# One-hot blocks of a token list: 24 packed blocks, one instruction each, in place of four instructions over a strided table

## The chip, the core and the metric

The kernel runs on one NeuronCore of a Trainium2 chip. TensorE (PE) multiplies matrices, VectorE (DVE) and ScalarE (ACT) work on elements, GpSimd (POOL) does elementwise work and issues the indirect DMAs, SyncE (SP) issues the other DMAs. The metric is the device time of one execution in microseconds (us), as a median of runs.

## The reference, cut to what matters

```python
attn_out = _attn_ref(q, k, v, f_logit)          # gated linear attention
x = moe(x)                                      # h = x @ w_in; leaky relu; @ w_out   (3072 x 384)
logits = x @ w_gate                             # 3072 tokens, 8 experts
for idx in np.argsort(-logits.flatten()):       # greedy, each expert takes at most 384 tokens
    tok, e = idx // 8, idx % 8
    if assigned[tok] < 0 and counts[e] < 384:
        assigned[tok] = e; counts[e] += 1
for e in range(8):
    out[assigned == e] = relu(x[assigned == e] @ w1[e]) @ w2[e]
```

The case is about the step between the last two loops: the tokens of an expert (a mask over 3072 tokens) have to become a list of 384 token numbers, by which rows are then gathered and scattered.

## The kernel before, in words

Tokens lie as 24 tiles (NT) of 128. The first layers run over groups of three tiles; the second half, which is the subject here, is started by `drv.run(layer2())` (line 1245). There a small driver interleaves generators while the program is written: `layer2` yields the large matmuls on PE (second layer `xp`, then for each of 8 experts 72 matmuls `hp` with the weights `w1e` and 72 matmuls `yp` with `w2e`, all 384 columns wide), and beside them run `routing()` and `lister()`. From line 1186 on the order on each engine is not the written one: a scheduler places the instructions by costs of its own, so an edit of one instruction's shape can move others.

`route` (line 649) finds the greedy assignment in seven rounds. A round has seven levels, and a level goes to and fro between DVE and PE: `c` (counts of the tokens by digit, PE), `cm`, `cd` (DVE), `cnt` (PE), `ok` (DVE), `tot` (PE), then `scr`, `J`, and the new mask `oh` (DVE), which the next `c` needs. A round ends with `ps`, sums over tokens that give each token of the finished expert its slot 1 to 384.

`token_list` (line 838) makes the list of one expert, and runs beside the first two levels of the next round; the last two lists are made after the last round. For each token it takes the slot's lower seven bits (`lob`) and its block 0 to 2 (`h3`, `rh`). `ohs` holds ones where a slot's number is `lob`, and 24 matmuls `pi` with `ohs` as weights and `rh` (six columns) as moving operand sum the token numbers into slot order. `ti`, `idx` and `row` turn them into integers. Then POOL gathers the rows (`xg`), and SP or PE turn them into `x2T`.

Before, `ohs` lies as [128, 128 slots, 24 tiles], made by four instructions of 32 slots each (line 858), against a constant `slots` of the same shape (line 618). The weights of tile j are then `oh[:, :, j]`: 128 elements that lie 24 elements apart.

```python
oh = rw.tile([128, 128, NT], BF16, name="ohs", bufs=1)
for a in range(4):
    b = slice(32 * a, 32 * a + 32)
    DVE.tensor_tensor(oh[:, b], lob[...].to_broadcast([128, 32, NT]), R["slots"][:, b], op=OP.is_equal)
    yield 600.0
for j in range(NT):
    mm(pi, oh[:, :, j], rh[:, :, j, :], j == 0, j == NT - 1)
```

All instructions are recorded by one helper (line 84), so the profile tells them apart by their tiles, not by their lines. PE, `hh`, `hl`, `hp`: `hh` and `hl` are the upper and lower halves of an expert's hidden values; part of `hl` is made on DVE and part on POOL.

Of the kernel before, what the change touches and what calls it, by code (L numbers as in the profile page):

```python
# [11 lines left out]
BF16 = mybir.dt.bfloat16  # L12
# [3 lines left out]
OP = mybir.AluOpType  # L16
# [75 lines left out]
def body(tc, qk, v, f_logit, w_in, w_out, w_gate, w1, w2, out):  # L92
    nc = tc.nc
    w_in, w_out = w_in.bitcast(I32), w_out.bitcast(I32)
    PE, DVE, ACT, POOL, SP = (InOrder(tc, e) for e in (nc.tensor, nc.vector, nc.scalar, nc.gpsimd, nc.sync))
# [6 lines left out]
    NT = B * S // 128  # L102
# [10 lines left out]
    with ExitStack() as ctx:  # L113
# [8 lines left out]
        def pool(c, name, side, bufs=1):  # L122
            return c.enter_context(tc.tile_pool(name=name, bufs=bufs, side=side, reuse_waits="tile"))
# [6 lines left out]
        def mm(o, l, r, start, stop):  # L130
            return PE.matmul(o, l, r, start=start, stop=stop, skip_group_check=True)
# [58 lines left out]
        def column_less_row(pool, tag):  # L190
            jp = pool.tile([128, 128], F32, name="jp", tag=tag)
            POOL.iota(jp, pattern=[[1, 128]], base=0, channel_multiplier=-1,
                      allow_small_or_imprecise_dtypes=True)
            return jp
# [390 lines left out]
        R = {}  # L585

        def route_constants():
            def const(name, shape, dt=F32):
                R[name] = rc.tile(shape, dt, name=name)
                return R[name]  # L590

            DVE.tensor_scalar(const("tri", [128, 128], BF16), column_less_row(rc, "jp"), 0.0, None, op0=OP.is_gt)
            DVE.memset(const("ones", [128, 128], BF16), 1.0)
            i128 = const("i128", [128, 128])
            POOL.iota(i128, pattern=[[1, 128]], base=0, channel_multiplier=0,
                      allow_small_or_imprecise_dtypes=True)
            const("place", [128, 384], F16)
            POOL.iota(const("i384", [128, 384]), pattern=[[1, 384]], base=1, channel_multiplier=0,
                      allow_small_or_imprecise_dtypes=True)
            DVE.tensor_scalar(const("i1", [128, 32]), i128[:, :32], 1.0, None, op0=OP.add)  # L600
            pi = const("pi", [128, 1], I32)
            DVE.tensor_copy(pi, pcol)
            for w in (4, 5):
                T, G = 2 ** w, 128 >> w
                thr = const(f"thr{w}", [128, NT // G, T, G], BF16)
                for a in range(NT // G):
                    DVE.tensor_copy(thr[:, a], R["i1"][:, :T, None].to_broadcast([128, T, G]))
                t = const(f"t{w}", [128, 1], I32)
                tf = const(f"tf{w}", [128, 1])
                DVE.tensor_scalar(t, pi, 7 - w, None, op0=OP.logical_shift_right)  # L610
                DVE.tensor_copy(tf, t)
                DVE.tensor_scalar(const(f"sel{w}", [128, T], F16), i128[:, :T], tf, None, op0=OP.is_equal)
                DVE.tensor_scalar(t, pi, G - 1, None, op0=OP.bitwise_and)
                DVE.tensor_copy(tf, t)
                d1 = const(f"d1{w}", [128, G])
                DVE.tensor_scalar(d1, i128[:, :G], tf, None, op0=OP.is_equal)
                DVE.tensor_copy(const(f"diag{w}", [128, E, G]), d1[:, None, :].to_broadcast([128, E, G]))
            DVE.tensor_copy(const("slots", [128, 128, NT], BF16), i128[:, :, None].to_broadcast([128, 128, NT]))
            wd = const("wd", [128, E])
            DVE.tensor_scalar(wd, i128[:, :E], -1.0, float(E), op0=OP.mult, op1=OP.add)  # L620
            DVE.tensor_copy(const("wdt", [128, NT, E], BF16), wd[:, None, :].to_broadcast([128, NT, E]))
            DVE.tensor_copy(const("wdx", [128, E, NT], BF16), wd[:, :, None].to_broadcast([128, E, NT]))
            DVE.tensor_scalar(const("wdc", [128, 1]), pcol, -1.0, float(E), op0=OP.mult, op1=OP.add)

            pw = const("pw", [128, 1], I32)
            DVE.tensor_scalar(pw, R["wdc"], 127.0, None, op0=OP.add)
            DVE.tensor_scalar(pw, pw, 23, None, op0=OP.logical_shift_left)
            DVE.tensor_scalar(const("bits", [E, 128], BF16), R["ones"][:E, :], pw.bitcast(F32)[:E], None, op0=OP.mult)
            jp3 = const("jp3", [128, 2, NT, 3])
            DVE.tensor_copy(jp3[:, 0], i128[:, :NT, None].to_broadcast([128, NT, 3]))  # L630
            DVE.tensor_copy(jp3[:, 1].rearrange("p a b -> p (a b)"), pcol.to_broadcast([128, NT * 3]))
            DVE.tensor_copy(const("i3", [128, NT, 3]), i128[:, None, :3].to_broadcast([128, NT, 3]))
            DVE.tensor_scalar(const("p1024", [128, 1]), pcol, float(E * 128), None, op0=OP.add)

            DVE.tensor_copy(const("opn", [128, E]), wd)
            DVE.memset(const("un", [128, NT]), 1.0)
            DVE.memset(const("asg", [128, NT]), 0.0)
            DVE.memset(const("kcap", [E, 1]), float(NT * 128 // E))
            DVE.memset(const("smx", [128, 1]), 0.0)

        def small(shape, name, dt=F32, bufs=2):
            return rw.tile(shape, dt, name=name, bufs=bufs)

        def bank(shape, name):
            return banks[0].tile(shape, F32, name=name, tag="rt", bufs=RT)
# [192 lines left out]
        def token_list(r, s):  # L838

            si = small([128, NT], "si", I32)  # L840
            DVE.tensor_scalar(si, s, -1.0, None, op0=OP.add)
            lo = small([128, NT], "lo", I32)
            DVE.tensor_scalar(lo, si, 127, None, op0=OP.bitwise_and)
            DVE.tensor_scalar(si, si, 7, None, op0=OP.arith_shift_right)
            lob = small([128, NT], "lob", BF16)
            DVE.tensor_copy(lob, lo)
            yield 300.0
            h3 = small([128, NT, 3], "h3")
            DVE.tensor_copy(h3, si[:, :, None].to_broadcast([128, NT, 3]))
            DVE.tensor_tensor(h3, h3, R["i3"], op=OP.is_equal)  # L850
            rh = small([128, 2, NT, 3], "rh", BF16)
            for a in range(2):
                DVE.tensor_tensor(rh[:, a], h3, R["jp3"][:, a], op=OP.mult)
            yield 300.0
            oh = rw.tile([128, 128, NT], BF16, name="ohs", bufs=1)
            for a in range(4):
                b = slice(32 * a, 32 * a + 32)
                DVE.tensor_tensor(oh[:, b], lob[:, None, :].to_broadcast([128, 32, NT]), R["slots"][:, b], op=OP.is_equal)
                yield 600.0
            pi = bank([128, 2, 3], "pi")  # L860
            for j in range(NT):
                mm(pi, oh[:, :, j], rh[:, :, j, :], j == 0, j == NT - 1)
            ti = small([128, 2, 3], "ti")
            DVE.tensor_copy(ti, pi)
            idx = rw.tile([128, 3], I32, name="idx", bufs=E)
            DVE.scalar_tensor_tensor(idx, ti[:, 0, :], 128.0, ti[:, 1, :], op0=OP.mult, op1=OP.add)

            row = rw.tile([128, 3], I32, name="row", bufs=E)
            if r:
                DVE.tensor_scalar(row, idx, 1.0, None, op0=OP.add)  # L870
            else:
                f = small([128, 3], "f3")
                DVE.tensor_scalar(f, idx, 1.0, None, op0=OP.add)
                DVE.scalar_tensor_tensor(row, f, float(NT * 128 - 128), f, op0=OP.is_le, op1=OP.mult)
                DVE.tensor_scalar(R["place"], R["i384"], s[:, NT - 1:NT], None, op0=OP.is_equal)
            LISTS["x", r] = row, idx
# [316 lines left out]
        rw = pool(ctxR, "rw", "right", 2)  # L1193
        cw = pool(ctxR, "cw", "right", 2)
        EW.append(pool(ctxR, "ew0", "right"))
        route_constants()
        zeros = rc.tile([128, 2 * Dm], BF16, name="zeros")
        POOL.memset(zeros, 0.0)
# [16 lines left out]
        def lister():  # L1215
            for _ in range(E):
                while not lists:
                    yield 300.0
                yield from token_list(*lists.pop(0))
# [65 lines left out]
```

## Time and profile before

| what | value |
|---|---|
| median of 3 runs | 860.26 us (860.1 to 863.48) |
| the profiled execution's own time | 859.49 us |
| its span | 857.7 us, 15968 instructions |
| PE matmul busy | 765.3 us, 89% of the span |
| DVE busy | 604.1 us, 70% |
| ACT, POOL busy | 360.8 us, 173.8 us |
| chain that ended last | PE 37%, DVE 29%, DMA 18%, issue 8%, ACT 5% |

The profiled execution lies 0.77 us below the median. Busy time of PE counts a matmul from its start to its modelled end, so neighbours overlap and the step from start to start is what one costs. The stretch from 535 us, where routing begins, to 767 us, where the last list is made, has routing and large matmuls mixed; after it only expert matmuls are left.

### The profile page before, as it was taken

How to read it: one execution, taken by the hardware profiler on the slowest of the kernel's cores; microseconds unless marked ns; L12 is line 12 of the kernel's file. 1: busy time of each engine (PE TensorE's matmuls, PEld its weight loads, DVE VectorE, ACT ScalarE, POOL GpSimd, SP SyncE). 2: the span in 40 equal slices, each digit the busy share in tenths (PEclk: the TensorE clock that was granted, in tenths of full speed). 3: DMA queues.
4: the chain of work that ended last, by engine and by line, in shares of the span. 5: the costliest groups of instructions: out<-in, count | busy, mean ns of one | idle time of the engine just before them, and what ended most of it. 6: DMA issues, size and time to landing. Idle time of an engine off the chain costs nothing.

```text
span 857.7 us, 15968 instructions
## 1 busy us (share of the span) xinstructions
PE 765.3 (89%) x6047; PEld 495.1 (58%) x6047; DVE 604.1 (70%) x1864; ACT 360.8 (42%) x760; POOL 173.8 (20%) x164
## 2 busy tenths in 40 slices
PE   6787767989889899899899999999989999989996
PEld 5664545757466566556556566555555555556663
DVE  6899999866865876776762566888798798861220
ACT  6556767555754755664551444000022122123321
POOL 5356654100000000000000000010243434445111
PEclk9879999999999999999999999999999999999999
DMA  9955454798786989798703530040277545535300
GB/s 235 235 138 148 149 138 123 188 252 257 231 254 213 273 252 254 223 241 232 212 10 64 108 54 2 20 166 21 62 231 195 149 143 171 172 151 179 135 28 28
DMA packets 102431, 135.93 MB, mean 158 GB/s; under 512 B 61905, under 2 KB 77266, under 8 KB 100306
## 3 DMA queue, kind: packets, MB, share of 16 engines
q1 hardware_dynamic: 96978, 100.31, 44.6%
q0 software_dynamic: 5376, 34.61, 11.6%
q8 instruction: 47, 0.77, 0.4%
q14 instruction: 30, 0.25, 0.1%
HBM read 86.52 MB, written 34.60 MB: 141 GB/s over the span
## 4 chain that ended last, share of the span: by engine, by line
PE 37%; DVE 29%; DMA 18%; issue 8%; ACT 5%; SPq 2%; POOL 1%; POOLq 0%; ACTq 0%; DVEq 0%
PE xp L84 11%; PE hp L84 10%; PE yp L84 8%; DMA w1d<-xw_o 7%; DMA w2d<-xw_o 5%; DVE xw_o L84 3%; DVE woutu L84 3%; DVE g L84 2%; ACT xw_o L84 2%; SPq L84 2%; DVE winu L84 2%; PE pi L84 2%; DVE St L84 1%; DVE am L84 1%; PE y L84 1%
## 5 line engine op out<-in xcount | busy, mean ns | idle before, releaser
L84 PE MATMUL hp<-xT,winh 128*128 128x384 f16 x768 | 194.1, 333 | 34.4 <-DVE g L84 34.2
L84 PE MATMUL xp<-wo,gh 128*128 128x384 f16 x768 | 196.0, 332 | 0.6 <-DVE g L84 0.6
L84 PE MATMUL hp<-xT,winl 128*128 128x384 f16 x384 | 127.5, 332 | 1.5 <-POOL winl L84 1.5
L84 PE MATMUL xp<-wo,gl 128*128 128x384 f16 x384 | 127.2, 331 | 0.0
L84 PEld LDWEIGHTS <-winh 128*128 128x128 f16 x768 | 75.3, 99 | 86.5 <-issue 45.9
L84 PEld LDWEIGHTS <-gh 128*128 128x128 f16 x912 | 83.4, 98 | 45.3 <-issue 3.9
L84 DVE SCALAR_TENSOR_TENSOR xw_o<-xw_s,xw_o 128x768 f16<-128x768 f32 x64 | 61.2, 956 | 67.4 <-ACT xw_o L84 63.7
L84 PE MATMUL hp<-x2T,w1e 128*128 128x384 f16 x576 | 99.6, 326 | 0.6 <-ACT x2T L84 0.4
L84 PE MATMUL yp<-w2e,hh 128*128 128x384 f16 x384 | 97.2, 327 | 0.0
L84 ACT ACTIVATE xw_o<-xw_s 128x768 f16<-128x768 f32 x64 | 54.0, 844 | 98.7 <-DMA w1d<-xw_o 41.8
L84 ACT ACTIVATE g<-hp 128x384 f32<-128x384 f32 x152 | 72.7, 484 | 24.4 <-PE hp L84 23.5
L84 DVE SCALAR_TENSOR_TENSOR g<-hp,g 128x384 f32<-128x384 f32 x128 | 69.4, 549 | 9.8 <-ACT g L84 9.3
L84 POOL IOTA jp<- 128x128 f32 x2 | 0.5, 238 | 371.1 <-PE hp L84 371.0
L84 PEld LDWEIGHTS <-w1e 128*128 128x128 f16 x576 | 54.1, 98 | 34.6 <-issue 1.2
L84 ACT ACTIVATE gh<-g 128x768 f16<-128x768 f32 x64 | 53.8, 841 | 31.1 <-DVE g L84 30.7
L84 ACT ACTIVATE hh<-hp 128x384 f16<-128x384 f32 x64 | 31.4, 491 | 77.4 <-PE hp L84 74.0
L84 DVE TENSOR_TENSOR gl<-g,gh 128x768 f16<-128x768 f32 x52 | 49.6, 955 | 20.2 <-ACT gh L84 20.1
L84 PE MATMUL yp<-w2e,hl 128*128 128x384 f16 x192 | 62.7, 327 | 0.0
L84 PEld LDWEIGHTS <-gl 128*128 128x128 f16 x528 | 47.5, 98 | 24.9 <-issue 1.4
L84 DVE SCALAR_TENSOR_TENSOR hl<-hp,hh 128x384 f16<-128x384 f32 x40 | 22.0, 551 | 44.9 <-ACT hh L84 44.8
L84 PEld LDWEIGHTS <-winl 128*128 128x128 f16 x384 | 38.2, 99 | 25.8 <-issue 2.2
L84 ACT ACTIVATE x<-xp 128x384 f16<-128x384 f32 x24 | 11.7, 485 | 96.9 <-PE xp L84 96.9
(248 smaller groups left out, 1362.0 us busy)
## 6 DMA issues: line engine op xcount, KB each, us to landing
xw_s<-in_moe_w SPq DMA_DIRECT2D x64, 384.0 KB, 4.0
w1d<-xw_o SPq DMA_DIRECT2D x32, 384.0 KB, 4.4
w2d<-xw_o SPq DMA_DIRECT2D x32, 384.0 KB, 4.3
qkT<-in_qk SPq DMA_DIRECT2D x48, 192.0 KB, 4.1
wout_s<-in_moe_w_out SPq DMA_DIRECT2D x16, 384.0 KB, 3.3
fT<-in_f_logit SPq DMA_DIRECT2D x24, 192.0 KB, 4.3
ld_v<-in_v SPq DMA_DIRECT2D x24, 192.0 KB, 4.2
x2d<-x SPq DMA_DIRECT2D x24, 192.0 KB, 2.9
```

The source lines that it names most:

```text
L84: i = f(*args, **kwargs)
```

## The change

Each tile's block of `ohs` is now made by an instruction of its own: `slots` is one row of 128 numbers, and `lob[:, j]` is a scalar per partition, kept in 32-bit floats. The block of tile j is then 128 neighbouring elements. There are 24 such instructions per list (before 4), 192 in all (before 32), and the table `slots` is 128 elements per partition (before 3072). The matmuls `pi` are the same in number and size.

```diff
-            DVE.tensor_copy(const("slots", [128, 128, NT], BF16), i128[:, :, None].to_broadcast([128, 128, NT]))
+            DVE.tensor_copy(const("slots", [128, 128], BF16), i128)
...
-            lob = small([128, NT], "lob", BF16)
+            lob = small([128, NT], "lob")
...
-            oh = rw.tile([128, 128, NT], BF16, name="ohs", bufs=1)
-            for a in range(4):
-                b = slice(32 * a, 32 * a + 32)
-                DVE.tensor_tensor(oh[:, b], lob[:, None, :].to_broadcast([128, 32, NT]), R["slots"][:, b], op=OP.is_equal)
-                yield 600.0
+
+            oh = rw.tile([128, NT, 128], BF16, name="ohs", bufs=1)
+            for j in range(NT):
+                DVE.tensor_scalar(oh[:, j], R["slots"], lob[:, j:j + 1], None, op0=OP.is_equal)
+                if j % 6 == 5:
+                    yield 600.0
             pi = bank([128, 2, 3], "pi")
             for j in range(NT):
-                mm(pi, oh[:, :, j], rh[:, :, j, :], j == 0, j == NT - 1)
+                mm(pi, oh[:, j], rh[:, :, j, :], j == 0, j == NT - 1)
```

The scheduler also places the rest anew. On DVE, beside the first level of the fifth round (the fourth list), this stood in a row before:

```order
L84 TENSOR_REDUCE cd<-cm 128x8
L84 TENSOR_TENSOR ohs<-lob,slots 128x768
L84 TENSOR_TENSOR rh<-h_8230,jp_6283 128x72 x2
L84 TENSOR_SCALAR ok<-cnt,kcap 8x32
L84 TENSOR_TENSOR ge<-dg,thr_6249 128x384
L84 TENSOR_TENSOR ohs<-lob,slots 128x768
L84 TENSOR_SCALAR scr,J<-tot 128x32
L84 TENSOR_SCALAR di<-key 128x24
L84 TENSOR_TENSOR ohs<-lob,slots 128x768
L84 SCALAR_TENSOR_TENSOR hl<-hp,hh 128x384
L84 SCALAR_TENSOR_TENSOR oh<-dg,J,oh 128x192
```

With the change this stands at the same place:

```order
L84 TENSOR_SCALAR ohs<-slots,lob 128x128 x4
L84 TENSOR_REDUCE cd<-cm 128x8
L84 TENSOR_SCALAR ohs<-slots,lob 128x128 x2
L84 SCALAR_TENSOR_TENSOR hl<-hp,hh 128x384
L84 TENSOR_SCALAR ohs<-slots,lob 128x128 x4
L84 TENSOR_SCALAR ok<-cnt,kcap 8x32
L84 TENSOR_SCALAR ohs<-slots,lob 128x128 x6
L84 TENSOR_SCALAR scr,J<-tot 128x32
L84 TENSOR_SCALAR di<-key 128x24
L84 TENSOR_SCALAR ohs<-slots,lob 128x128
L84 SCALAR_TENSOR_TENSOR oh<-dg,J,oh 128x192
```

Six blocks now stand ahead of `cd`, six ahead of `ok`, six ahead of `scr` and one ahead of `oh`; the other five come after `oh`. One `ge` and one `hl` have left this piece.

On PE, the 24 `pi` of that list stood in one run before, between large matmuls:

```order
L84 LDWEIGHTS w1e
L84 MATMUL hp<-x2T,w1e 128x384
L84 LDWEIGHTS ohs
L84 MATMUL pi<-rh,ohs 128x6
L84 LDWEIGHTS ohs
L84 MATMUL pi<-rh,ohs 128x6
```

With the change 14 stand in a run behind `tot`, and then one each between large matmuls (`yp`, the expert's second product):

```order
L84 LDWEIGHTS ohs
L84 MATMUL pi<-rh,ohs 128x6
L84 LDWEIGHTS hh
L84 MATMUL yp<-w2e,hh 128x384
L84 LDWEIGHTS ohs
L84 MATMUL pi<-rh,ohs 128x6
L84 LDWEIGHTS hl
L84 MATMUL yp<-w2e,hl 128x384
```

The run is broken up, and each `pi` now has its own block to wait for. Over all lists 83 of the 192 `pi` stand alone between large matmuls. Between the `c` of the first level and the `cnt` of the second stood 34 large matmuls for this list, and now stand 40; over rounds two to seven a round has about 12 more than before, and behind the last list 133 stand ahead of expert 6 where 201 stood.

## Rows read from the trace of the kernel before

**Rows 1.** The page's head: span, then busy time, share and instructions by engine.

```profile
span 857.7 us, 15968 instructions
PE 765.3 (89%) x6047; PEld 495.1 (58%) x6047; DVE 604.1 (70%) x1864; ACT 360.8 (42%) x760; POOL 173.8 (20%) x164
```

**Rows 2.** Waits of PE, 530 to 770 us: total us, times, longest us.

```profile
PE c L84 <- DVE oh L84: 5.8, 5, 1.6
PE ps L84 <- DVE x L84: 1.9, 2, 1.7
...
PE pi L84 <- DVE ohs L84: 0.9, 1, 0.9
```

**Rows 3.** The tile ohs: count, ns min/median/max, first and last start, shape.

```profile
L84 PEld LDWEIGHTS <-ohs x192: 147/184/193, 571.5 to 767.2; 128*128 128x128 bf16 x192
...
L84 DVE TENSOR_TENSOR ohs<-lob,slots x32: 535/546/552, 567.9 to 765.1; 128x768 bf16<-128x768 bf16 x32
```

**Rows 4.** Timeline of PE around the fourth list: start us, us, operation, count, idle before.

```profile
661.28 0.30 PE L84 MATMUL c<-oh,ge 128*128 128x32 bf16 x6 [1.57 <-DVE oh L84]
661.43 1.79 PE L84 MATMUL hp<-x2T,w1e 128*128 128x384 f16 x10
663.17 0.18 PE L84 MATMUL cnt<-sel,cd 128*8 128x32 f16 x1
663.28 1.15 PE L84 MATMUL hp<-x2T,w1e 128*128 128x384 f16 x6
...
664.48 1.47 PE L84 MATMUL hp<-x2T,w1e 128*128 128x384 f16 x8
666.09 1.84 PE L84 MATMUL pi<-rh,ohs 128*128 128x6 bf16 x24
667.79 0.65 PE L84 MATMUL hp<-x2T,w1e 128*128 128x384 f16 x3
668.27 0.30 PE L84 MATMUL c<-oh,ge 128*128 128x32 bf16 x6
```

**Rows 5.** The chain that ended last: a run of small matmuls with packed weights.

```profile
509.47 2.24 PE lp L84 x90
```

**Rows 6.** Timeline of DVE: the routing constants, and two small instructions of a round.

```profile
531.51 2.02 DVE L84 CAST slots<-i 128x3072 bf16<-128x3072 f32 x1
...
538.05 0.24 DVE L84 TENSOR_SCALAR bits<-ones,pw 8x128 bf16<-8x128 bf16 x1
538.21 0.18 DVE L84 COPY i<-i 128x72 f32<-128x72 f32 x1
...
654.81 0.23 DVE L84 TENSOR_SCALAR es<-wd,mx 128x8 f32<-128x8 f32 x1
654.94 0.20 DVE L84 TENSOR_SCALAR k<-wdc,mx 8x1 f32<-8x1 f32 x1
```

**Rows 7.** One stretch: us, busy of PE, PEld, DVE, ACT, POOL; clock, DMA, GB/s.

```profile
661.28:669.65 8.37, 8.23 (x72) 5.13 (x71) 7.37 (x36) 2.23 (x5) 2.05 (x2) 1.00 0.01 3
```

**Rows 8.** Timeline of DVE in that stretch.

```profile
663.96 0.34 DVE L84 TENSOR_TENSOR ge<-dg,thr 128x384 bf16<-128x384 bf16 x1
664.22 0.54 DVE L84 TENSOR_TENSOR ohs<-lob,slots 128x768 bf16<-128x768 bf16 x1
...
664.80 0.77 DVE L84 TENSOR_SCALAR di<-key 128x24 int32<-128x24 int32 x1
665.49 0.55 DVE L84 TENSOR_TENSOR ohs<-lob,slots 128x768 bf16<-128x768 bf16 x1
665.96 0.54 DVE L84 SCALAR_TENSOR_TENSOR hl<-hp,hh 128x384 f16<-128x384 f32 x1
666.42 0.41 DVE L84 SCALAR_TENSOR_TENSOR oh<-dg,J,oh 128x192 bf16<-128x192 bf16 x1
```

**Rows 9.** Timeline of POOL in that stretch.

```profile
663.88 1.66 POOL L84 TENSOR_TENSOR hl<-g,hh 128x384 f16<-128x384 f32 x1 [3.85 <-ACT g L84]
```

**Rows 10.** Timeline of PE at the seventh list.

```profile
761.12 1.81 PE L84 MATMUL pi<-rh,ohs 128*128 128x6 bf16 x24 [0.92 <-DVE ohs L84]
```

## The prediction, made before the change was timed

> **What bounds the kernel now.** I read the page's head first, then PE's waits from 530 to 770 us, where routing runs, then PE and DVE side by side around one token list. The head shows PE as the busiest engine, 765.3 of 857.7 us [rows 1]. In the routing stretch PE nearly always has a large matmul to run, and what it loses are a few waits of one kind: `c` for the mask `oh` that opens a round, 5.8 us in 5 waits, `ps` 1.9 us, `pi` for `ohs` 0.9 us [rows 2]. Behind the last list only expert matmuls are left. So the time is PE's work plus those waits: a nanosecond less on PE counts in full, and an instruction more on DVE counts only where it makes PE wait. The reader should look in the timelines at starts, not at durations: neighbouring instructions overlap, and the step from one start to the next is the price.
>
> **PE: the `pi` matmuls.** The weights of `pi` come from elements 24 apart, and one load of them takes 184 ns at the median [rows 3]. The fourth list's 24 `pi` start at 666.09 and the next matmul at 667.79 [rows 4]: 1.70 us, 71 ns each. The eight lists are alike. Small matmuls with packed weights of the same 128 by 128 shape step much faster: six `c` from 661.28 to 661.43, 25 ns each [rows 4], and 90 `lp` in 2.24 us, also 25 ns [rows 5]. The change makes each block packed and leaves the moving operand alone. Bounds: 71 ns (nothing gained, if not the spacing but something else about `pi` is slow) and 25 ns. I take 25, since `c` is nearest in type, shape and number of moving columns: 24 times 25 is 0.60 us, 1.10 less per list, **8.8 us less over 8 lists**.
>
> A rule speaks against this. The Trainium skill, page "TensorE: Matmul & The Clock Gate", section "Weight-path perf modes — Fast Weight Load (FWL) and DoubleRow", says that the fast load applies to 128 weights that are not FP32, "packed or strided", for a step up to 1,024 elements. By it a step of 24 costs nothing and this term would be 0. The trace speaks the other way, 71 against 25 ns, though it holds no third case that would show spacing alone to be the reason.
>
> **DVE: 24 instructions for 4.** An old `ohs` instruction steps 0.47 us (665.49 to 665.96 [rows 8]), four are 1.88 us. The new form (bf16 in and out, 128 elements, one scalar per partition) occurs once in the trace, as `bits`: it starts at 538.05 and the next instruction at 538.21 [rows 6], 0.16 us. That it covers only 8 partitions and multiplies is the difference. Bounds: 0.13 us, the step of `es` with 8 elements (654.81 to 654.94 [rows 6]), and 0.24 us, the whole duration of `bits`, if neighbours that write one tile did not overlap. I take 0.16, the same form: 24 times that is 3.84 us, **1.96 us more on DVE per list** (bounds 1.24 and 3.88).
>
> The page "VectorE: DVE Perf Modes" of the Trainium skill, section "The TRN2 errata — SBUF-src ops pay a fixed extra latency per instruction", warns of just this cut: many small tiles each pay the fixed part. Its measured fixed part of about 150 cycles would make it, as an estimate from that page, (150 + 128/4)/0.96 GHz = 0.19 us an instruction, 2.7 us more per list, and a time of about 856 us. The row of `bits` is lower, and I follow the row.
>
> **Does that reach PE?** Take the stretch from the fourth list's first `c` to the second level's `cnt`, 8.37 us, in which DVE was busy 7.37 [rows 7]. With the change DVE has 1.96 more there, while the order moves one `hl` (665.96 to 666.42, 0.46) and one `ge` (663.96 to 664.22, 0.26 [rows 8]) out of it: 8.61 us. In it is a stall: `di` at 664.80 takes until 665.49, 0.69 us where `es` steps 0.13 [rows 6], and it ends with the POOL instruction that began at 663.88 and ran 1.66 [rows 8, 9]. Without the stall it is 8.0 us. PE has in the same stretch of the new order 40 large matmuls at 0.16 (three from 667.79 to 668.27 [rows 4]), 6.4 us; 12 `c` and 24 `pi` at 25 ns, 0.9; `cnt` and `tot`, 0.25 each: ten matmuls from 661.43 would end at 663.03, `cnt` starts at 663.17 and its follower at 663.28 [rows 4]. Together 7.8 us. So the two engines come out about level, because the scheduler has put six more large matmuls there; what PE loses anew is a POOL stall of 0.6 us per list. I charge it to all six lists that run beside a round: **3.6 us more** (0 if POOL falls elsewhere).
>
> **Waits that go.** The fourth list's `pi` run waited: eight matmuls from 664.48 end at 665.76, `pi` starts at 666.09 [rows 4], 0.3 us, and lists three to six are alike. With 14 blocks early and the others spread out, that wait is paid for by the cover above: 1.2 us less. The seventh list's wait of 0.92 us [rows 10] goes too, as only the first block has to be there when the first `pi` comes. Together **2.1 us less**. Between `ps` and the first `c` of a round the new order has 12 more large matmuls over five rounds, 1.9 us more cover for the 5.8 us of waits for `oh` [rows 2]; since one more `hl` of 0.46 us [rows 8] stands in that chain in places, I count **1.0 us less**.
>
> **Nothing.** The `slots` table shrinks from a 2.02 us instruction [rows 6] by 24 times in elements; PE shows no wait on DVE at that place, so its cover is the queue of large matmuls there, 0; if that cover were gone it would be a gain of at most 2. In the last two lists a `pi` and the large matmul beside it take 0.16 + 0.025 = 0.185 us on PE, and DVE's 0.16 per block stays ahead: 0. POOL's queue is reordered, with a gather of tokens now behind a weight load; experts 1 to 5 get their tokens an expert's length ahead, and the last lists still have 133 large matmuls (21 us) ahead of expert 6: 0. SP's queue is the same.
>
> **Sum.** -8.8 + 3.6 - 2.1 - 1.0 = -8.3 us. The sum is made against the profiled execution: 859.49 - 8.3 = 851.2. That execution lies 0.8 below the median of the runs, so I expect 852.0.
>
> **The rivals.**
>
> DVE takes the place of the bound (slower). The point from which it decides is 0.16 us per block, at which the two engines are about level. At the upper bound of 0.24 each of six lists gets 24 times 0.08 = 1.9 us longer, 11.5 us, and in the last two lists 48 times (0.24 - 0.185) = 2.6: 852.0 + 14.1 = 866 us. For it: one row of 8 partitions carries the price. Against it: DVE steps are shorter than durations everywhere in these rows. 8%. A milder form, 0.20 us, costs six times 0.96 and gives 857.8 us: 12%.
>
> A lone `pi` costs as much as a lone `cnt` (slower). `cnt` between large matmuls costs 0.25 us, not 25 ns [rows 4]. If that came from standing alone behind a wait of its own, 83 lone `pi` would cost 83 times 0.225 = 18.7 us more: 871 us. Against it: `cnt` loads 8 columns of weights and `c` 128; `c` waits for `oh` as well, and the run at 668.27 steps off without a gap [rows 4]; `pi` has the full shape. 6%.
>
> The change does not make `pi` faster. The spacing is not what makes the weight load slow, 8.8 us stay, and the rest nets out at +0.5: 860.8 us. The skill's rule on the fast load (above) says this. Against it the 184 ns of the load itself [rows 3]. 8%.
>
> **How the numbers follow.** The forecast has 66%. A measurement of this kernel can tell about 0.5% (4.3 us) from no change, so faster means below 856.0. The forecast and a quarter of the milder form lie there: 69%. The other three quarters (9%) and the rule (8%) lie within: 17%. The two slower rivals: 14%. Low end: without the new stalls 848.4, and with the full 1.9 us of cover 847.5. The high end takes in the milder form and the rule, 861.5; outside are the two slower rivals and a tail of the forecast. The forecast's own range is 847.5 to 856.
>
> **What would show it.** In the profile of the changed kernel: 192 weight loads of `ohs` near 100 ns, runs of `pi` that step 25 ns, `ohs` instructions that step 0.16 us, PE's waits for `ohs`, `cd` and `oh` in sum no more than 1 us a round above those of before, and the seventh list without its 0.92 us. Steps of `ohs` over 0.2 us, or gaps of 0.1 us on both sides of a lone `pi`, would make the prediction wrong.

## The result, and the profile after

The changed kernel took **851.95 us** (median of 4 runs, 850.13 to 852.39), the kernel before 860.94 us beside it (4 runs, 860.1 to 863.48): ratio 0.9893, 95% interval 0.9856 to 0.9931. On a second chip, with 12 and 23 runs, the ratio was 0.9908 (0.9879 to 0.9936), which is 8 us. The forecast was 852.0.

The page's head of the changed kernel, against [rows 1]:

```profile
span 848.4 us, 16128 instructions
PE 760.3 (90%) x6047; PEld 488.2 (58%) x6047; DVE 615.0 (72%) x2024; ACT 360.7 (43%) x760; POOL 171.4 (20%) x164
```

PE is busy 5 us less, DVE 10.9 us more. Next the tile `ohs` (count, ns min/median/max, first and last start, shape), against [rows 3]:

```profile
L84 DVE TENSOR_SCALAR ohs<-slots,lob x192: 233/242/1491, 563.2 to 768.4; 128x128 bf16<-128x128 bf16 x192
L84 PEld LDWEIGHTS <-ohs x192: 94/95/100, 566.4 to 768.9; 128*128 128x128 bf16 x192
```

A load takes 95 ns in place of 184. The longest of the small DVE instructions lasted 1.49 us, six times the median; what that is comes below. PE's timeline at the fourth list (start us, us, operation, count, idle before it), against [rows 4]:

```profile
659.61 0.30 PE L84 MATMUL c<-oh,ge 128*128 128x32 bf16 x6 [1.39 <-DVE oh L84]
...
662.78 0.18 PE L84 MATMUL cnt<-sel,cd 128*8 128x32 f16 x1 [0.91 <-DVE cd L84]
...
664.74 0.51 PE L84 MATMUL pi<-rh,ohs 128*128 128x6 bf16 x14
665.11 0.32 PE L84 MATMUL yp<-w2e,hh 128*128 128x384 f16 x1
665.27 0.17 PE L84 MATMUL pi<-rh,ohs 128*128 128x6 bf16 x1
665.29 0.32 PE L84 MATMUL yp<-w2e,hl 128*128 128x384 f16 x1
```

Fourteen `pi` start at 664.74 and the next matmul at 665.11: 26 ns each, before 71. A `pi` that stands alone between large matmuls takes 0.02 us, from 665.27 to 665.29. The same rows show what is new: `cnt` waits 0.91 us for `cd`, where before it waited for nothing. PE's waits from 530 to 770 us in sum (total us, times, longest us), against [rows 2]:

```profile
PE c L84 <- DVE oh L84: 5.5, 7, 1.7
PE cnt L84 <- DVE cd L84: 3.1, 4, 1.2
PE ps L84 <- DVE x L84: 1.4, 3, 0.5
PE c L84 <- DVE ge L84: 0.6, 1, 0.6
PE pi L84 <- DVE rh L84: 0.5, 1, 0.5
PE pi L84 <- DVE ohs L84: 0.2, 1, 0.2
```

With a last row of 0.2 us (`hp` for `x2T`) that is 11.5 us. Before, the same view adds up to 10.3, with the 0.2 of `x2T` and a row that [rows 2] leaves out:

```profile
PE c L84 <- DVE ge L84: 1.5, 1, 1.5
```

The view leaves out waits of 0.15 us and less. The gain is PE work that went, less a little more waiting.

**Where in the span.** Here is each kernel cut at its last `lp`, the last matmul of the logits (us; then busy time and count of PE, PEld, DVE, ACT, POOL; clock, DMA share, GB/s). The part after it holds all of routing, the lists and the experts. Before:

```profile
0.00:534.90 534.90, 461.92 (x3880) 318.64 (x3881) 392.09 (x674) 300.25 (x630) 84.47 (x76) 0.96 0.67 180
534.90:857.70 322.80, 303.38 (x2173) 176.44 (x2170) 211.99 (x1190) 60.54 (x130) 89.33 (x88) 0.99 0.39 123
```

After:

```profile
0.00:531.01 531.01, 463.13 (x3876) 318.57 (x3876) 390.68 (x681) 300.23 (x630) 84.50 (x76) 0.96 0.67 181
531.01:848.40 317.39, 297.14 (x2178) 169.64 (x2174) 224.33 (x1344) 60.50 (x130) 86.93 (x88) 1.00 0.41 125
```

Of the 9.3 us between the two spans only 5.4 lie in the second part, and 6.2 if one counts that the new order has moved five large `xp` (0.16 us each) behind the last `lp`. The other 3 us lie ahead of it, where PE runs the same instructions but for those five. That part scatters: in eight kernels of this study with the same PE instructions in the same order there, the changed one among them, it took from 528.3 to 535.0 us; in the three kernels with the order of before it took from 532.9 to 534.9. So the second part is what I set side by side below, and medians where they are close enough. The second part scatters too: two executions of the changed kernel took 317.39 and 318.06 us.

### The profile page after: what moved, and what is told of

Same layout as the page of the kernel before. It is cut to its first block, busy times and chain, and to the rows that moved or that the text cites. A ratio compares the mean times of both kernels' runs of the same rounds, so it can differ in the third digit from the quotient of the medians.

```text
span 848.4 us, 16128 instructions
## 1 busy us (share of the span) xinstructions
PE 760.3 (90%) x6047; PEld 488.2 (58%) x6047; DVE 615.0 (72%) x2024; ACT 360.7 (43%) x760; POOL 171.4 (20%) x164
## 4 chain that ended last, share of the span: by engine, by line
PE 36%; DVE 29%; DMA 17%; issue 9%; ACT 4%; SPq 3%; POOL 1%; POOLq 0%; ACTq 0%; DVEq 0%
PE xp L84 11%; PE hp L84 11%; DMA w1d<-xw_o 8%; PE yp L84 8%; DMA w2d<-xw_o 5%; DVE woutu L84 3%; DVE xw_o L84 3%; DVE winu L84 3%; SPq L84 3%; DVE g L84 2%; ACT xw_o L84 2%; DVE am L84 1%; DVE St L84 1%; DMA turned<-x 1%; PE y L84 1%
## 5 line engine op out<-in xcount | busy, mean ns | idle before, releaser
L84 PE MATMUL hp<-xT,winh 128*128 128x384 f16 x768 | 196.9, 337 | 37.1 <-DVE g L84 35.5
L84 PE MATMUL xp<-wo,gh 128*128 128x384 f16 x768 | 193.9, 330 | 0.8 <-DVE g L84 0.8
L84 PE MATMUL hp<-xT,winl 128*128 128x384 f16 x384 | 129.4, 337 | 0.6 <-POOL winl L84 0.6
L84 PE MATMUL hp<-x2T,w1e 128*128 128x384 f16 x576 | 102.5, 326 | 0.7 <-ACT x2T L84 0.4
L84 ACT ACTIVATE x<-yp 128x384 f32<-128x384 f32 x24 | 11.8, 490 | 99.1 <-PE yp L84 91.8
```

Of the source, the lines that this page charges most:

```text
L84: i = f(*args, **kwargs)
```

## Experiments

### The weights' distance or the new order: five kernels

**24 instructions, blocks as before.** The changed kernel, but with the old layout:

```diff
-            oh = rw.tile([128, NT, 128], BF16, name="ohs", bufs=1)
+            oh = rw.tile([128, 128, NT], BF16, name="ohs", bufs=1)
...
-                DVE.tensor_scalar(oh[:, j], R["slots"], lob[:, j:j + 1], None, op0=OP.is_equal)
+                DVE.tensor_scalar(oh[:, :, j], R["slots"], lob[:, j:j + 1], None, op0=OP.is_equal)
...
-                mm(pi, oh[:, j], rh[:, :, j, :], j == 0, j == NT - 1)
+                mm(pi, oh[:, :, j], rh[:, :, j, :], j == 0, j == NT - 1)
```

> 24 instructions a list as in the changed kernel, but each writes its block at a distance of 24 elements, so that the weights lie as before. Theory (the gain is the packed weights of pi; the many small instructions cost only some new waits): loads of ohs near 184 ns, runs of pi step 71 ns, and the 8.8 us come back: about 860.8 us, or more if a write at a distance makes an instruction dearer than 0.16 us. Rival (the gain comes from the new order and from blocks that are ready one by one, the spacing of the weights doesn't matter): the time stays near 852 us.

868.13 us, 1.0139 of before (1.0089 to 1.019). Runs of `pi` stepped 71 to 72 ns again, though each block is ready by itself, so the finer blocks are not what makes `pi` fast. But the run changes two things: the writes on DVE became dear as well. In the timeline of DVE 14 blocks take 5.04 us to the next start, 0.36 us each against 0.16:

```profile
783.90 5.47 DVE L84 TENSOR_SCALAR ohs<-slots,lob 128x128 bf16<-128x128 bf16 x14
788.94 0.80 DVE L84 SCALAR_TENSOR_TENSOR hl<-hp,hh 128x384 f16<-128x384 f32 x1
```

By the step of `pi` the rival is refuted; the time holds both prices and prices neither.

**Old instructions, packed output.** The kernel before, whose four instructions write to packed blocks:

```diff
-                DVE.tensor_tensor(oh[:, b], lob[:, None, :].to_broadcast([128, 32, NT]), R["slots"][:, b], op=OP.is_equal)
+                DVE.tensor_tensor(oh[:, :, b].rearrange("p j s -> p s j"), lob[:, None, :].to_broadcast([128, 32, NT]), R["slots"][:, b], op=OP.is_equal)
```

> The kernel before with one thing changed: its four instructions write the same elements to packed blocks, so that the output is written at a distance of 128 elements and the inputs are read as before. Theory: pi steps 25 ns, 8.8 us less; if the write at a distance costs nothing on DVE (0.47 us an instruction) the time is 860.9 - 8.8 - 1 to 2 of waits that go = 850 to 851 us; if it doubles the instruction (0.92 us, 1.8 us more a list) about as the changed kernel, 852 us. Rival (the gain of the change was the order with single blocks): 860 us, since here a list's pi still wait for the last of four instructions.

942.51 us, 1.0986 of before (1.0941 to 1.1032): far outside both expectations. The tile `ohs` shows why:

```profile
L84 PEld LDWEIGHTS <-ohs x192: 95/104/117, 580.9 to 859.7; 128*128 128x128 bf16 x192
...
L84 DVE TENSOR_TENSOR ohs<-lob,slots x32: 3535/3570/4091, 565.9 to 855.2; 128x768 bf16<-128x768 bf16 x32
```

The weights load fast, as expected, but a write at a distance of 128 elements costs DVE 3.57 us an instruction where 0.55 was the duration before [rows 3]. PE then waited 16.5 us for `ohs`, 13.6 for `ok` and 7.9 for `cd`. From 540 us on PE's mean granted clock was 0.88, against 0.99 in the kernel before, which adds to the time: from 571.2 to 578.1 us, behind a wait of 2.5 us for `cd`, it was at the lower of its two levels (1.2 GHz), and large matmuls there stepped 0.32 us in place of 0.16. The run can't price `pi`; it shows that the layout can't be had for nothing from the old instruction.

**One distance per list.** The changed kernel with blocks interleaved by n:

```diff
+            n = (24, 12, 8, 4, 2, 1, 6, 3)[r]
+            oh = rw.tile([128, NT // n, 128, n], BF16, name="ohs", bufs=1)
...
+                DVE.tensor_scalar(oh[:, j // n, :, j % n], R["slots"], lob[:, j:j + 1], None, op0=OP.is_equal)
...
+                mm(pi, oh[:, j // n, :, j % n], rh[:, :, j, :], j == 0, j == NT - 1)
```

> The changed kernel, with another distance between the weights of a block in each list: 24, 12, 8, 4, 2, 1, 6 and 3 elements for the first to the eighth list. Theory (the distance makes the load slow): the list with 1 steps 25 ns, the one with 24 71 ns, the ones between rise with the distance. If by a straight line (2 ns for each element), the lists cost 1.1, 0.5, 0.35, 0.15, 0.05, 0, 0.25 and 0.1 us more, 2.5 us in all: 854.5 us; if any distance over 1 costs all of it, 7.7 us more: 859.7 us. Rival (the distance doesn't matter, as a rule of the Trainium skill has it, page TensorE: Matmul & The Clock Gate, section Weight-path perf modes: packed or strided): all lists step 25 ns and the time is 852 us.

856.22 us, 0.9999 of before (0.9977 to 1.002). PE's timeline, the first run of `pi` in the lists with distances 24, 8, 4, 2 and 1, each with the matmul that follows:

```profile
564.89 0.99 PE L84 MATMUL pi<-rh,ohs 128*128 128x6 bf16 x12
565.74 0.32 PE L84 MATMUL xp<-wo,gl 128*128 128x384 f16 x1
...
636.39 0.90 PE L84 MATMUL pi<-rh,ohs 128*128 128x6 bf16 x12
637.15 0.32 PE L84 MATMUL yp<-w2e,hh 128*128 128x384 f16 x1
...
670.56 0.56 PE L84 MATMUL pi<-rh,ohs 128*128 128x6 bf16 x12
670.98 0.32 PE L84 MATMUL yp<-w2e,hh 128*128 128x384 f16 x1
...
703.78 0.46 PE L84 MATMUL pi<-rh,ohs 128*128 128x6 bf16 x12
704.10 0.32 PE L84 MATMUL yp<-w2e,hl 128*128 128x384 f16 x1
...
736.89 0.48 PE L84 MATMUL pi<-rh,ohs 128*128 128x6 bf16 x13
737.24 0.32 PE L84 MATMUL yp<-w2e,hh 128*128 128x384 f16 x1
```

From start to start that is 71, 63, 35, 27 and 27 ns. With the loads and DVE's instructions of the same lists (medians of their durations):

| distance, elements | load, ns | `pi` in a run, ns | DVE per block, duration ns |
|---|---|---|---|
| 1 | 96 | 27 | 242 |
| 2 | 97 | 27 | 300 |
| 3 | 103 | none in a run | 325 |
| 4 | 114 | 35 | 369 |
| 6 | 124 | none in a run | 542 |
| 8 | 146 | 63 | 676 |
| 12 | 151 | 61 | 686 |
| 24 | 150 | 71 | 686 |

Each distance has one list of its own, at its own place in the kernel. So it is the distance, neither by a straight line nor at once: 2 costs PE nothing, 4 a fifth and 8 four fifths of what 24 costs. That the distance doesn't matter is refuted for these weights. By its ratio the kernel is 8 us over the changed one, more than the 2.5 of the straight line, but DVE's column rises too, so the time doesn't price PE's part; the next two kernels do.

**Zeros added, nothing else moved.** Two kernels, the same to the last instruction in their order; only where the zeros lie differs:

```diff
+            POOL.memset(const("nil", [128, NT, 128], BF16), 0.0)
...
-                mm(pi, oh[:, j], rh[:, :, j, :], j == 0, j == NT - 1)
+                mm(pi, oh[:, j], rh[:, :, j, :], j == 0, False)
+                mm(pi, R["nil"][:, j], rh[:, :, j, :], False, j == NT - 1)
```

In the second of them the table is `[128, 128, NT]` and the weights are `R["nil"][:, :, j]`.

> The changed kernel with 24 more matmuls of pi's form a list, whose weights are a packed constant block of zeros (they add 0). Their order is the same as in the next run to the last instruction. Theory (PE's time counts in full, 25 ns each): 192 times 25 ns = 4.8 us over the changed kernel. Rival (in these stretches DVE sets the time): less than 2 us over it.

> The same, with the zeros' weights 24 elements apart; DVE does just what it does in the run before. Theory (distance alone makes a pi step 71 ns where 25 would do, and PE's time counts in full): 192 times 46 ns = 8.8 us over the run with packed zeros, 13.6 over the changed kernel. Rival A (the distance doesn't matter to the load, the skill's rule): the same as with packed zeros. Rival B (half of it is hidden where PE waits for DVE anyway): 4 us over the run with packed zeros.

Medians 860.42 and 868.99 us, 0.9995 (0.9958 to 1.0031) and 1.0102 (1.0047 to 1.0156) of before on the same chip. The second parts, first packed, then strided:

```profile
538.24:861.40 323.16, 302.69 (x2370) 174.97 (x2366) 224.63 (x1345) 60.54 (x130) 85.93 (x88) 0.99 0.38 123
```

```profile
537.04:869.60 332.56, 312.56 (x2370) 183.70 (x2366) 224.76 (x1345) 60.50 (x130) 86.12 (x88) 0.98 0.37 120
```

DVE, ACT and POOL are busy the same to 0.2 us; PE is busy 9.9 us longer, and the stretch takes 9.4 longer (at 0.98 of the clock against 0.99). The medians differ by 8.6. Expected were 8.8, against 4 and 0 for the rivals. That is the clean price of the distance: by the medians 45 ns a `pi`, by the second parts 49, where 46 were expected, and all of it is in the time. The packed zeros lie 5.1 us over the changed kernel's second part on that chip (318.06 us), where 4.8 were expected. By the medians they lie 8.6 over it: the part ahead is longer too (538.24 us), where POOL now clears the table in 2.7 us and an `lp` waits 2.1 us for `gl`. What else makes it longer is not shown.

### DVE's price, or POOL: seven kernels

**The changed kernel again**, on the second chip, for comparison:

> The changed kernel unedited, on the same chip as the next three, so that they can be set beside it. All theories: 0.989 of the kernel before, as measured first.

851.81 us, 0.9908 (0.9879 to 0.9936). PE waited 6.0 us for `oh` and 3.2 for `cd`, where the first execution has 5.5 and 3.1; the waits belong to the kernel.

**Four instructions for packed blocks**, with the token's number repeated along the row (`lob` is in bf16 again):

```diff
+            for a in range(4):
+                t = slice(6 * a, 6 * a + 6)
+                DVE.tensor_tensor(oh[:, t], lob[:, t, None].to_broadcast([128, 6, 128]), R["slots"][:, None, :].to_broadcast([128, 6, 128]), op=OP.is_equal)
+                yield 600.0
```

> Packed blocks as in the changed kernel, but made by four instructions of six tiles each, in which the token's number is repeated along the row (distance 0). pi should step 25 ns as in the changed kernel. DVE: between 0.47 us an instruction (as the old ones) and 0.92 us (hl takes 0.46 us for 384 elements, twice that for 768), 1.9 to 3.7 us a list against 3.9 with 24 instructions. Theory (the 24 instructions cost PE the new waits for cd, some 3.5 us): 848.5 us at the low price, 852 us at the high one. Rival (DVE's extra work is hidden, the new waits come from the order): 852 us whatever the price.

846.64 us on a chip where before took 855.92: 0.9901 (0.9872 to 0.9931), level with the changed kernel. Each instruction takes 0.946 us (median), the high price, and at that price both theories expected just this: the run can't tell them apart. By its second part, 315.21 us, it is 2.2 to 2.9 under the changed kernel, with 10.2 us of waits.

**Blocks in pairs**, so that the inner run is two neighbouring elements. The edit is against the kernel before, and `slots` becomes `[128, 128, 2]`:

```diff
+            oh = rw.tile([128, NT // 2, 128, 2], BF16, name="ohs", bufs=1)
+            lp = lob.rearrange("p (a b) -> p a b", b=2)
+            for a in range(4):
+                t = slice(3 * a, 3 * a + 3)
+                DVE.tensor_tensor(oh[:, t], lp[:, t, None, :].to_broadcast([128, 3, 128, 2]), R["slots"][:, None].to_broadcast([128, 3, 128, 2]), op=OP.is_equal)
+                yield 600.0
...
+                mm(pi, oh[:, j // 2, :, j % 2], rh[:, :, j, :], j == 0, j == NT - 1)
```

> Blocks in pairs: two tiles alternate, so that the weights of one lie 2 elements apart (in the run on distances such a list still stepped 27 ns), and four instructions a list make them, whose inner run is two neighbouring elements. DVE: between 0.47 us an instruction (the old one, inner run 24) and 0.9 us (the packed one with a repeated number). Theory (DVE's extra work makes PE's new waits for cd, 3.1 us in the changed kernel): at 0.47 us those waits go and the time is some 3 us under the changed kernel, 0.985 to 0.986 of before; at 0.9 us level with it, 0.989. Rival (the new waits come from the order, DVE's price doesn't matter): 0.989 at either price.

849.82 us, 0.9873 (0.9827 to 0.9919). The tile `ohs` shows the price of before and packed loads at once:

```profile
L84 PEld LDWEIGHTS <-ohs x192: 96/96/101, 569.3 to 758.8; 128*128 128x128 bf16 x192
...
L84 DVE TENSOR_TENSOR ohs<-lob,slots x32: 534/553/1277, 567.2 to 758.0; 128x768 bf16<-128x768 bf16 x32
```

DVE has 2 us less to do per list, but PE's waits stay (4.4 for `oh`, 2.6 for `cd`, 1.6 for `x`, 1.4 for `ok`, 11.9 in all with the small ones). The second part is 316.22 us, 1.2 to 1.8 under the changed kernel, half of what the theory expected; the interval of the ratio holds both expectations. By the waits, DVE's price is not what makes them.

**Twelve spare instructions more per list:**

```diff
+                if j % 2:
+                    DVE.tensor_scalar(rw.tile([128, NT, 128], BF16, name="spare", bufs=1)[:, 0], R["slots"], lob[:, j:j + 1], None, op0=OP.is_equal)
```

> The changed kernel with 12 more instructions of the new form a list, which write to a tile that nobody reads: 12 times 0.16 = 1.96 us more on DVE a list, as much as the change itself added. Theory of the prediction (DVE and PE are about level beside a list): each of it counts in the six lists beside a round, 11.8 us, and some 3 us more in the last two lists: 14 to 15 us over the changed kernel, 1.007 of before. Rival (DVE still has slack there, the waits come from the order and from POOL): under 3 us over the changed kernel, at most 0.994.

855.58 us, 0.9939 (0.9902 to 0.9977); second part 321.57 us, some 4 us over the changed kernel. By the ratios it is 2.7 us over the changed kernel on the second chip. DVE's busy time rose by 19 us, and at most a fifth of it reached the end. That is at the rival's bound of 3 us, and far from 14 to 15.

**hl on DVE.** In the rows of the changed kernel the waits for `cd` come where POOL makes an `hl`. DVE's timeline, then POOL's, then PE's, at the third list (`xg` is a gather of tokens):

```profile
626.14 0.22 DVE L84 TENSOR_TENSOR h<-h,i 128x72 f32<-128x72 f32 x1
626.29 1.49 DVE L84 TENSOR_SCALAR ohs<-slots,lob 128x128 bf16<-128x128 bf16 x1
627.70 0.36 DVE L84 TENSOR_TENSOR rh<-h,jp 128x72 bf16<-128x72 f32 x2
...
628.64 0.17 DVE L84 TENSOR_REDUCE cd<-cm 128x8 f16<-128x32 f16 x1
```

```profile
625.83 0.95 POOL L84 DMA_INDIRECT xg<-x2d,row  x1 [0.30 <-issue]
626.79 0.92 POOL L84 TENSOR_TENSOR hl<-g,hh 128x384 f16<-128x384 f32 x1
```

```profile
628.86 0.18 PE L84 MATMUL cnt<-sel,cd 128*8 128x32 f16 x1 [1.23 <-DVE cd L84]
```

The block of 0.16 us lasts 1.41 to the next start, until POOL is done at 627.71. It began half a microsecond before the `hl`, while POOL made the gather. It is no single case: from 530 us on, 20 DVE instructions of the changed kernel lasted over 0.2 us longer than the median of their form, 11.5 us in all; 17 of them ran beside an `hl` on POOL, and the other three, 0.7 us together, beside a gather. In the kernel before there were 22, 14.4 us in all, 20 of them beside an `hl`.

This experiment makes all of `hl` on DVE:

```diff
-                    if f % 2 == 0 and r < E - 2:
+                    if False:
```

> The changed kernel with all of hl made on DVE (0.46 us each) and none on POOL, 24 of them beside the routing. Theory (the new waits for cd and the waits for oh follow on stalls of DVE while a POOL hl of 0.95 us runs): the stalls of 0.6 to 0.9 us go, 0.46 comes for each, and with them most of the 3.1 us for cd and a part of the 5.5 us for oh: 2 to 4 us under the changed kernel. Rival (DVE is what PE waits for, whatever fills it): 24 times 0.46 = 11 us more on DVE, which show as 3 to 10 us over the changed kernel.

**842.52 us**, 0.9798 of before (0.9752 to 0.9843). PE's waits from 530 to 770 us, all of them:

```profile
PE c L84 <- DVE oh L84: 0.9, 3, 0.4
PE ps L84 <- DVE x L84: 0.4, 1, 0.4
PE c L84 <- DVE ge L84: 0.4, 2, 0.2
PE pi L84 <- DVE rh L84: 0.3, 1, 0.3
PE hp L84 <- DVE x2T L84: 0.2, 1, 0.2
```

2.2 us in place of 11.5. DVE makes 24 more `hl`, and is busy for 615.8 us where it was 615.0:

```profile
PE 760.7 (91%) x6047; PEld 490.7 (58%) x6047; DVE 615.8 (73%) x2048; ACT 352.1 (42%) x736; POOL 148.5 (18%) x140
```

What the 24 `hl` add, the stalls had taken: three long DVE instructions are left, 0.6 us in all. The second part is 306.70 us, 10.7 less, more than the 2 to 4 expected, since I had taken only the waits for `cd` and a part of those for `oh` for POOL's. The edit changes more than `hl`: ACT no longer makes the 24 `g` from which POOL made it (8.6 us of its busy time), and the scheduler placed PE's and DVE's instructions anew. The 9.3 us of waits all ended on DVE, none on ACT; what the new order gave is not priced, and 1.4 of the 10.7 us lie outside these waits.

**The same with pairs**, and **the kernel before with hl on DVE**:

> Both: blocks in pairs by four instructions a list, and hl on DVE. By the theory of stalls the gains add: some 3 us under the run with pairs alone, 0.983 to 0.984 of before. By the rival 0.990 or more.

839.08 us, 0.978 (0.9742 to 0.9819), the fastest of the study; its second part is 306.05 us. With no stalls the pairs add 0.65 us there, which can't be told from nothing. It lies 11.3 us under the changed kernel, where the two alone lay 10.7 and 1.2 to 1.8 under it, so the gains add but for about 1 us; neither expected ratio was met, since both were reckoned from too small a gain for `hl`.

> The kernel before (blocks over the strided table, four instructions a list) with all of hl on DVE, as in the run of the changed kernel with hl on DVE, in which PE waited 2.2 us in all for the routing. Set beside that run it prices the change alone where DVE is no longer stalled. Theory (packed weights are worth 8.8 us, DVE's 24 instructions are hidden now): 8.8 us over that run, that is 0.990 of before, and about 315.5 us from the last matmul of the logits to the end against 306.7 there. Rival (a part of the change's gain was the order and the finer blocks, and goes with the stalls): 4 us over that run or less, 0.985.

849.88 us, 0.9902 (0.9873 to 0.993), as the theory had it. Of PE's 5.8 us of waits for `oh` [rows 2] this is left:

```profile
PE c L84 <- DVE oh L84: 0.8, 3, 0.5
```

The second parts of the two kernels with `hl` on DVE, first with the blocks of before, then with those of the change:

```profile
534.59:849.80 315.21, 304.52 (x2173) 177.21 (x2170) 211.65 (x1214) 51.31 (x106) 63.49 (x64) 0.99 0.40 126
```

```profile
533.10:839.80 306.70, 295.76 (x2178) 169.53 (x2174) 224.39 (x1368) 51.42 (x106) 64.09 (x64) 0.99 0.40 129
```

8.5 us apart, though five `xp` more lie in the second (9.3 with them counted), with PE's waits 1.8 and 2.2 us: 8.8 us less PE busy time, 12.7 more DVE busy time. The first shows whole in the time, the second not at all.

## Why the prediction was right, and where not

**The `pi` matmuls, -8.8: right** in cause, and in size where they are priced alone: 26 ns in the changed kernel's rows; 8.6 us between the medians of the two kernels with zeros; 8.5 between the two with `hl` on DVE. In the change itself it was less. Added up from each start to the next in the two second parts, the steps of all 192 `pi` fell from 13.3 to 5.9 us, 7.4 less: the old ones stepped 69 ns on average and not 71, and the new runs have 0.8 us of gaps in them.

A rule spoke against this term: the Trainium skill, page "TensorE: Matmul & The Clock Gate", section "Weight-path perf modes — Fast Weight Load (FWL) and DoubleRow", has the fast load for weights "packed or strided", for steps up to 1,024 elements. Taken as in the prediction, that a step of 24 costs nothing, it would have had the table above flat. The loads in it rise from 96 to 150 ns, so the measurement decides against that reading for this form of weights.

**DVE's 0.16 us per block: right.** 22 blocks run from 760.11 to 763.70, 163 ns each. The estimate of 0.19 from the Trainium skill, page "VectorE: DVE Perf Modes", section "The TRN2 errata — SBUF-src ops pay a fixed extra latency per instruction", was a sixth too high for the step.

**The new waits, +3.6: right in size and half right in cause.** The view has 3.1 us for `cd`. By the steps (what each is over the usual step of the matmul that begins it, summed by the matmul that comes next) PE lost 3.6 us more ahead of `cnt` than before. I charged a POOL stall, because DVE and PE came out level beside a list. The stall is real: without POOL's `hl` the wait for `cd` is gone. That the two engines are level is not: 1.96 us more per list cost 3 to 4 us where "level" means 14 to 15, and 2 us less per list gained 1 to 2. The slower rival in which DVE becomes the bound was priced by the same mistake, and so too dear.

**The waits that go, -2.1 and -1.0: somewhat too large, and the second wrong in cause.** By the steps PE lost 1.5 us less ahead of a `pi` that follows other work (the seventh list's 0.92 us became 0.5, now for `rh`) and 0.8 us less ahead of `c`. But the view has the waits for `oh` fall only from 5.8 to 5.5 us, and the one for `ge` from 1.5 to 0.6. The step that failed was to read the 5.8 us for `oh` [rows 2] as a long chain on DVE, which 12 large matmuls more would cover. It counts five rounds only: ahead of the fourth round 31 large matmuls stand where 38 stood, so the cover grew by five in all. And these waits were mostly POOL stalls: in the kernel before with `hl` on DVE 0.8 us of them are left. That 0.8 us came out is luck.

**The sum, -8.3: 2 us too much for what the change did to the second part.** That part gives -6.2 us with the five `xp` counted; by the steps -7.4 + 3.6 - 1.5 - 0.8 make -6.1. The medians give -9.0 and -8.1, with intervals that reach from -12.4 to -5.5. What of the part ahead of the last `lp` belongs to the change, if anything, stays open. That the median hit the forecast to 0.1 us is luck by about 2 us.

**A lone `pi` at 0.25 us: refuted** by the rows above, 0.02 us.

## What to carry to other kernels

Where the same small matrix is written by one engine and loaded as weights by PE, look at the distance between its elements on both sides: try 1 or 2, and keep it on the writing side too. When PE waits for DVE, look first whether DVE's late instruction lasts far longer than its like, and what POOL runs at that time; counting DVE's instructions told little here, taking 24 off POOL took nearly all of the waits away. And cut the spans of two profiles at a point up to which both run the same work, before giving their difference to a change.

## What the runs showed that I had not expected

- Writes on DVE at a distance: a block of 128 took 242 ns packed, 369 at 4 elements, 676 at 8 and hardly more beyond (686 at 12 and at 24); 768 elements at a distance of 128 took 3.57 us against 0.55.
- A repeated number along the row (distance 0) made the four instructions 0.946 us long, pairs of neighbours 0.553.
- While POOL made a gather and then an `hl` of 0.92 us, one DVE instruction of 0.16 us lasted 1.41, and ended with the `hl`. Of the 24 `hl` 17 had such a DVE instruction beside them. With these `hl` on DVE, 9.3 of the 11.5 us that PE waited were gone.
- A lone `pi` with strided weights was not always dear: in the list with distance 24 the pair of a `pi` and a large matmul took 0.19 us in some places (566.22 to 566.41) and 0.29 in others (569.00 to 569.29); in the lists with 1, 2 and 4 it took 0.19 everywhere. What tells them apart wasn't tried.
